# The last two batches of an attention-and-MoE kernel: first layer in three groups of 384 tokens in place of four of 288

## The chip, the core and the metric

The kernel runs on one core of a Trainium2 chip. The metric is the device time of one execution in microseconds (us); the time before is the median of three runs. A core has a matrix engine (TensorE, in the profile PE for the matmuls and PEld for the loads of their stationary operand), a vector engine (VectorE, DVE), a scalar engine (ScalarE, ACT), GpSimd (POOL), and SyncE (SP), which here issues all DMAs. Matmuls write to PSUM, eight banks of 512 fp32 columns in each of 128 partitions.

## The reference, cut

Four batches of 576 tokens with 8 heads of 64 pass a memory attention, then two MoE layers over all 2304 tokens:

```python
a = softmax(phi)                        # over 32 memory slots
k_m, v_m = a^T k, a^T v                 # per head: 32 x 64
attn = softmax(q k_m^T / 8) v_m         # per head: 576 x 64
x = attn as 2304 x 512
x = leaky_relu(x @ w_in) @ w_out        # first layer: 512 -> 2048 -> 512
out = mish(x @ w_in2) @ w_out2          # second layer
```

All inputs and the output are fp32.

## The kernel before

Every fp32 operand of the large matmuls is split into two float32r parts, hi and lo, and a product is three matmuls (hi hi, lo hi, hi lo) that add up in one PSUM bank. v_m is multiplied into w_in beforehand (the tiles vw, made in `vw_tasks`), so that the first layer's hidden block of 128 features needs, for a group of tokens, 2 head groups x 3 = 6 matmuls of vw on the attention weights `at`; that bank is h_t.

`stage1` writes one item: a group of 288 tokens (`NB1`, half a batch; `sub` is the half) and one block m of 128 of the 2048 hidden features. PE does the 6 matmuls into h_t (line 1226). ACT takes the leaky ReLU of it twice, as float32r (hi_t) and as fp32 (e_t, line 1240), and DVE subtracts the two (lo_t, line 1247). PE then multiplies with w_out (line 1259): for each of 4 blocks of 128 outputs, a PSUM bank acc_t each, hi with both parts of w_out (8 matmuls) and lo with the hi part (4 matmuls). An item is thus 18 matmuls, each with its own weight load and 288 columns. After the 16 items of a group the four acc_t are copied out as x_t or at_t (lines 312, 310 and 1304) and the next group takes the banks.

The first two batches pass in a turn that follows the decoding of the weights. The last two, which the change touches, pass group by group: batch 2 half 0, batch 2 half 1, batch 3 half 0, batch 3 half 1, 16 items each. What comes between them on PE is the attention of the next batch and its vw tiles (line 975: for a chunk of 512 features 8 small fp32 matmuls, which a trace shows as 16 records), copied to hi and lo by ACT and DVE (lines 310, 312 and 326). There are 8 vw buffers (`vw_tag`), 2 for each chunk of a batch.

The second layer (lines 1579 and 1791) works on groups of 384 tokens. Its operand is built by `split_x` on DVE and ACT in buffers `xt` that lie where the attention's buffers lay, so `split_x(0)` waits for the last user of those (`apool_users`, to which `keep` adds a task).

No order is written out by hand. Each piece of work is a task with the engines that may do it, an estimated cost and a priority, which is its place in a count of items; `Order.run` plays the tasks against the estimates and emits an instruction when its engine, its inputs and its buffers are free. K holds the offsets: S2 is the distance between the two halves of a batch's scores, XL how many items before the end of the first layer `split_x(0)` becomes due. The estimate for n matmuls of N columns is

```python
def mm(n, count=1):
    return count * (n / 2400 + 0.0133)
```

Of the kernel before, what the change touches and what calls it, by code (L numbers as in the profile page):

```python
# [23 lines left out]
def hop(a, b):  # L24
# [5 lines left out]

K = dict(
    LAG1=2, WIN=8, OB=2, RS=4, FILL=58, A1=10, S1=8.0,
    A2=30, S2=2.6, V1=2.4, V2=14, W2=45, W2S=3.8, O='phi0 kv0 phi1 q0 w0 kv1 q1 w1 w2 w3', HF0=-20.0, HF1=-7.0,
    HFD=0.3, TOP=0.1, HI=0.2, WO=2.0, WOL=1, WC=3.0, WC0=-38.0, V0=3.0, COLD=20, GL=1.5, AL=5.0, XL=22.0, T='0:1 0:1 1:2 0:2 1:2', SB=1,
    DW=280e3, DQ=1.3, DP=1.2, DS=0.78, DI=0.38, L4=0.5, L4P=1.6, L4S=0.8, L4T=5.0, MA=6, QL=4, PL=6, BH=(9,3,3,3,3), FK=-52.5, DWF=0.85, MV="......rvvrrvvrvr",
)

# [122 lines left out]
def kernel(  # L160
# [791 lines left out]

    win, win_ready, w_scr, w_loads = {}, {}, {}, [[] for _ in range(NC)]

    def vw_tasks(b, c, p0):
# [26 lines left out]

        t = keep(add(
            {"PE": 1.2}, p0, f, [x for g in range(NG) for x in vT[b, g][1] + win_ready[b, c, g]],
            pss + us, [vT[b, g][0] for g in range(NG)] + wbs,
        ))
        for g in range(NG):
            u, ps_b = us[g], pss[g]
            th, tl = hi_lo(
                p0 + 0.5 * g + 0.2, 512, lambda u=u: u.t[:, 0], lambda u=u: u.t[:, 1], lambda ps_b=ps_b: ps_b.t,  # L990
                [t], (), [u, ps_b], ps=True,
            )
            vw[b, c, g] = (u, th, tl)


# [70 lines left out]
    def next_batch(b):  # L1066
        d, st = (K["A1"], K["S1"]) if b == 1 else (K["A2"], K["S2"])
        p = base[b] - d
        kv_rest(b, p, 0.08 * d / 2)
        score_rest(b, p + 0.1 * d, (p + 0.3 * d, p + 0.3 * d + st), 0.03 * d)  # L1070

    def next_vw(b, c):
        vw_tasks(b, c, at_item["1", b, 0, 4 * c] - (K["V1"] if b == 1 else K["V2"]))

    for b, cs in chunk_turns:
        if b and not cs[0]:
            next_batch(b)
        for c in cs:
            if b:
                next_vw(b, c)  # L1080
                continue
            w_chunk(c)
            for m in range(4 * c, 4 * c + 4):
                wo_unit(m)


    kv_again = [kvq.new([P, 2, 1024]) for _ in range(2)]
    opened = [add({"SP": 0.0}, K["W2"], lambda e, x=x: x.make(), (), [x]) for x in kv_again]

    class View:  # L1090

# [14 lines left out]
            b.make = make  # L1106
            return b

    views = [View(j) for j in range(3)]
# [102 lines left out]
    def passes(n):  # L1212
        return [(j, wi) for j in range(n) for wi in range(2)]

    def stage1(i, b, sub, m):
        cols = slice(sub * NB1, (sub + 1) * NB1)
        c, j0 = m // 4, (m % 4) * P
        h = h_tag.new([P, NB1])
        us, ats = [vw[b, c, g] for g in range(NG)], [at[b, g] for g in range(NG)]
# [12 lines left out]
        t1 = add(  # L1232
            {"PE": mm(NB1, 6)}, i, f1, [x for u in us for x in u[1:]] + [x for u in ats for x in u[1 + sub]], [h],
            [u[0] for u in us + ats],
        )
        t1.main = i
        eb, hb, lb = e_tag.new([P, NB1]), hi_tag.new([P, NB1], F32R), lo_tag.new([P, NB1], F32R)

        def lrelu(o):
            nc.scalar.activation(out=o, in_=h.t, func=AF.Prelu, alpha=0.01)  # L1240


        t4 = add({"ACT": act(NB1, True)}, i + 0.3, lambda e: lrelu(hb.make()), [t1], [hb], [h])
        t3 = add({"ACT": act(NB1, True)}, i + 0.4, lambda e: lrelu(eb.make()), [t1, t4], [eb], [h])
        t5 = add(
            {"DVE": dve(NB1)}, i + 0.6,
            lambda e: nc.vector.tensor_tensor(out=lb.make(), in0=eb.t, in1=hb.t.bitcast(F32), op=ALU.subtract),  # L1247
            [t4, t3], [lb], [eb, hb],
        )
        first, last = m in firsts(b), m + 1 in firsts(b) + [NM]  # L1250
        if first:
            for kk in range(NK):
                accs[kk] = acc_tag.new([P, NB1])
        ac = dict(accs)
        wu = wo[m]

# [11 lines left out]
        if first:  # L1268
            for kk in range(NK):
# [13 lines left out]
        if last:  # L1283
            for kk in range(NK):
                tl = add(
                    {"PE": mm(NB1)}, i + LAG1 + 0.1 + 0.01 * kk, lambda e, kk=kk: mms([(kk, 0, 1)]),
                    [t5, *hs], (), [lb, wu[0], ac[kk]],
                )
                key = (b, kk // 2)
                fresh = key not in x1  # L1290
                if fresh:
                    if b < B - 1:
                        x1[key] = [x1_tag.new([P, 2, S]), {}]
                    else:
# [12 lines left out]

                deps = [tl] + [x for x in list(evs.values())[:1]]
                if add_in:
                    deps.append(evs[kk, sub])  # L1310
                evs[kk, sub] = add(
                    {"DVE": dve(NB1)} if add_in else {"ACT": act(NB1, True), "DVE": dve(NB1)},
                    i + LAG1 + 0.2, fe, deps, [xb] if fresh else [], [ac[kk]] if fresh else [ac[kk], xb],
                )
# [15 lines left out]

    slots = [
        (base[B - 1] + NM + x, t) for x, _, t in sorted(
            [(LAG1 + m, 0, wo_tag) for m in range(NM)] + [(4 * c + 3, 1, vw_tag) for c in range(NC) for _ in range(2)],
            key=lambda x: x[:2],
        )
    ]  # L1340
# [555 lines left out]
```

## Time and profile before

| | |
|---|---|
| median of 3 runs | 742.09 us (741.64 to 742.65) |
| the profiled execution | 741.87 us |
| its span, first to last instruction | 740.1 us |
| granted TensorE clock over the span | 0.999 |
| PE busy | 731.0 us, 99% of the span, 5875 matmul records |
| ACT, DVE busy | 402.5 us (54%), 550.6 us (74%) |
| first layer of batches 2 and 3 on PE, with what lies between | ends near 382 us |

The busy time of PE is the time in which at least one matmul is under way. Consecutive matmuls overlap, so the mean duration of one (297 ns for 288 columns) is not what one more of them costs. That is the distance from one start to the next in a dense stretch, called the pitch below: the length of a stretch divided by its matmuls.

### The profile page before, as it was taken

What the parts mean: (1) busy time and instruction counts of PE and PEld (TensorE: products, weight loads), DVE (VectorE), ACT (ScalarE), POOL (GpSimd) and SP (SyncE); (2) the same over time, 40 slices, a digit from 0 to 9 for tenths busy, and PEclk for the clock granted to TensorE, in tenths of its full rate; (3) what the DMA queues carried; (4) which work ended last, traced back from release to release, by engine and by line L of the source; (5) the groups of instructions that cost most, each with busy time, mean ns of one, the idle gap of its engine ahead of it and who ended that gap; (6) DMA issues with size and microseconds to landing.
All of it is one profiled execution on the core that took longest, in us unless ns stands there. A gap on an engine that the chain in (4) does not pass through costs nothing.

```text
span 740.1 us, 15587 instructions
## 1 busy us (share of the span) xinstructions
PE 731.0 (99%) x5875; PEld 701.3 (95%) x5875; DVE 550.6 (74%) x1153; ACT 402.5 (54%) x877; POOL 0.7 (0%) x6
## 2 busy tenths in 40 slices
PE   8999999999999999999999999999999999999997
PEld 7788899888999989999999999999999999999997
DVE  6899868598766965647859797867777966775595
ACT  4866458565553775645546665544464644444442
POOL 0000000000000000000000000000000000000000
PEclk9999999999999999999999999999999999999999
DMA  9793957787869587863559898788988778996475
GB/s 353 299 318 115 350 172 232 229 274 229 290 207 286 171 274 269 262 233 101 199 199 338 302 312 254 233 271 249 300 278 264 250 239 258 297 290 207 126 218 182
DMA packets 99322, 183.73 MB, mean 248 GB/s; under 512 B 8112, under 2 KB 51376, under 8 KB 99248
## 3 DMA queue, kind: packets, MB, share of 16 engines
q1 hardware_dynamic: 99248, 182.75, 75.5%
q8 instruction: 46, 0.75, 0.4%
q14 instruction: 28, 0.23, 0.1%
HBM read 140.25 MB, written 42.47 MB: 247 GB/s over the span
## 4 chain that ended last, share of the span: by engine, by line
PE 96%; DVE 2%; ACT 1%; DMA 0%; issue 0%
PE acc_t L1259 28%; PE h_t L1579 22%; PE acc_t L1791 22%; PE h_t L1226 13%; PE misc_t L1791 2%; PE misc_t L975 2%; PE acc_t L1579 2%; PE acc_t L508 1%; PE misc_t L741 1%; PE misc_t L646 1%; DMA phi_t<-in_phi_dram 0%; PE h_t L865 0%; ACT raws_t L369 0%; ACT raws_t L374 0%; PE misc_t L689 0%
## 5 line engine op out<-in xcount | busy, mean ns | idle before, releaser
L1259 PE MATMUL acc_t<-hi_t,wo_t 128*128 128x288 f32 x1024 | 160.6, 297 | 0.4 <-DVE x_t L312 0.3
L1259 PEld LDWEIGHTS acc_t<-hi_t,wo_t 128*128 128x128 f32 x1024 | 142.9, 188 | 12.2 <-issue 7.0
L1226 PE MATMUL h_t<-at_t,vw_t 128*128 128x288 f32 x768 | 123.1, 296 | 0.0
L1791 PE MATMUL acc_t<-hi_t,wo_t 128*128 128x384 f32 x448 | 114.4, 336 | 0.0
L1240 ACT ACTIVATE hi_t<-h_t 128x288 fp32r<-128x288 f32 x128 | 52.6, 411 | 111.8 <-PE acc_t L1259 105.3
L1226 PEld LDWEIGHTS h_t<-at_t,vw_t 128*128 128x128 f32 x768 | 108.5, 188 | 0.7 <-issue 0.6
L1247 DVE TENSOR_TENSOR lo_t<-e_t,hi_t 128x288 fp32r<-128x288 f32 x128 | 57.3, 450 | 47.4 <-ACT e_t L1240 21.6
L1259 PE MATMUL acc_t<-lo_t,wo_t 128*128 128x288 f32 x512 | 89.8, 297 | 0.5 <-DVE lo_t L1247 0.5
L1791 PEld LDWEIGHTS acc_t<-hi_t,wo_t 128*128 128x128 f32 x448 | 81.3, 188 | 0.0
L1259 PEld LDWEIGHTS acc_t<-lo_t,wo_t 128*128 128x128 f32 x512 | 74.7, 188 | 6.3 <-issue 5.6
L1579 PE MATMUL h_t<-xt_t,vw_t 128*128 128x384 f32 x396 | 79.4, 336 | 0.0
L1579 PE MATMUL h_t<-xt_t,wo_t 128*128 128x384 f32 x352 | 75.8, 336 | 0.0
L1791 PE MATMUL acc_t<-lo_t,wo_t 128*128 128x384 f32 x224 | 75.6, 337 | 0.0
L1758 DVE TENSOR_TENSOR lo_t<-wo_t,hi_t 128x384 fp32r<-128x384 f32 x94 | 52.0, 554 | 31.4 <-ACT hi_t L310 29.9
L1579 PEld LDWEIGHTS h_t<-xt_t,vw_t 128*128 128x128 f32 x396 | 69.3, 188 | 0.0
L310 ACT ACTIVATE hi_t<-wo_t 128x384 fp32r<-128x384 f32 x78 | 40.7, 524 | 40.7 <-PE acc_t L1791 36.4
L1579 PEld LDWEIGHTS h_t<-xt_t,wo_t 128*128 128x128 f32 x352 | 61.9, 188 | 0.0
L1240 ACT ACTIVATE e_t<-h_t 128x288 f32<-128x288 f32 x128 | 52.0, 406 | 0.0
L1791 PE MATMUL acc_t<-wo_t,hi_t 128*128 128x256 f32 x240 | 45.0, 282 | 0.0
L1604 ACT ACTIVATE wo_t<-wo_t 128x384 f32<-128x384 f32 x53 | 27.6, 522 | 30.8 <-DVE wo_t L1598 30.6
L1791 PEld LDWEIGHTS acc_t<-lo_t,wo_t 128*128 128x128 f32 x224 | 42.0, 188 | 0.0
L310 ACT ACTIVATE wo_t<-h_t 128x384 f32<-128x384 f32 x50 | 24.5, 489 | 31.1 <-PE h_t L1579 31.1
(263 smaller groups left out, 1110.0 us busy)
## 6 DMA issues: line engine op xcount, KB each, us to landing
wo_t<-tscr SPq DMA_DIRECT2D x168, 256.0 KB, 3.8
vw_t<-wsum SPq DMA_DIRECT2D x32, 512.0 KB, 4.7
win_t<-wscr SPq DMA_DIRECT2D x24, 512.0 KB, 5.5
raw_t<-in_moe_w_in_dram SPq DMA_DIRECT2D x19, 512.0 KB, 7.5
raw_t<-in_moe_w_out_dram SPq DMA_DIRECT2D x17, 512.0 KB, 5.5
wsum<-vw_t SPq DMA_DIRECT2D x16, 512.0 KB, 4.5
wo_t<-wsum SPq DMA_DIRECT2D x16, 512.0 KB, 4.3
tscr<-raw_t SPq DMA_DIRECT2D x9, 512.0 KB, 5.5
```

The source lines that it names most:

```text
L310: nc.scalar.activation(out=o, in_=i, func=AF.Copy)
L508: nc.tensor.matmul(out=acc.t[rows, :].rearrange("p (j d) -> p j d", j=2), lhsT=phv()[rows, r, :], rhs=kv.t[rows, :2304].rearrange("p (j r ...
L646: nc.tensor.matmul(out=accs_[g].t[o:o + M, :].rearrange("p (j d) -> p j d", j=2), lhsT=ph.t[rows, x, j, :], rhs=kv[g].t[rows, :, x % 2, j, :],
L975: nc.tensor.matmul(out=pss[g].t[M * (h ^ g):M * (h ^ g) + M, :], lhsT=vT[b, g][0].t[rows, g, h ^ g if b else h // 2, :], rhs=wbs[g].t[rows ...
L1226: nc.tensor.matmul(out=h.t, lhsT=us[g][0].t[:, wi, j0:j0 + P], rhs=ats[g][0].t[:, ai, cols], start=(n == 0), stop=(n == 3 * NG - 1),)
L1240: nc.scalar.activation(out=o, in_=h.t, func=AF.Prelu, alpha=0.01)
L1247: lambda e: nc.vector.tensor_tensor(out=lb.make(), in0=eb.t, in1=hb.t.bitcast(F32), op=ALU.subtract),
L1259: nc.tensor.matmul(out=ac[kk].t, lhsT=wu[0].t[:, wi, kk * P:(kk + 1) * P], rhs=(hb if src == 0 else lb).t, start=(first and (wi, src) == ( ...
L1579: nc.tensor.matmul(out=h.t, lhsT=w[:, wi, c0:c0 + P], rhs=xp[b, xi].ap()[:, j], start=(first and j == 0 and k3 == 0), stop=(j == 1 and k3 ...
L1604: lambda e: nc.scalar.activation(out=t_of[x](), in_=h.t if h else t_of[x](), func=AF.Mish),
L1758: lambda e, hb=hb, lb=lb, src=src: nc.vector.tensor_tensor(out=lb.make(), in0=src(), in1=hb.t.bitcast(F32), op=ALU.subtract),
L1791: nc.tensor.matmul(out=ac[t].t, lhsT=T[:, wi, t * P:(t + 1) * P] if wide else x.t[:, t * P:(t + 1) * P], rhs=x.t if wide else T[:, wi], st ...
```

## The change

The 64 items of 288 tokens of batches 2 and 3 become 48 items of 384 (`NB2`): group 0 is tokens 0 to 383 of batch 2, group 1 is the last 192 of batch 2 and the first 192 of batch 3, group 2 is tokens 192 to 575 of batch 3. The two parts of group 1 need different stationary tiles, so its items write h_t in two pieces of 192 columns with 6 matmuls each; from there on the item is one of 384 columns.

Group 1 needs the vw tiles of both batches. Chunk 0 of batch 3 goes into buffers of the attention (phi and the two T1, wrapped by `Two`); chunks 1 to 3 take the buffers of batch 2's chunks 0 to 2 once group 1 is through with them. The attention of batch 3 becomes due earlier with it, S2 and XL are new numbers (XL, in the same dict, goes from 22.0 to 18.0), and the places in which the second layer's tiles become free are renumbered. Nothing of batches 0 and 1 or of the second layer's matmuls is changed.

```diff
 K = dict(
-    A2=30, S2=2.6, V1=2.4, V2=14, W2=45, W2S=3.8, O='phi0 kv0 phi1 q0 w0 kv1 q1 w1 w2 w3', HF0=-20.0, HF1=-7.0,
...
+    A2=30, S2=3.5, V1=2.4, V2=14, W2=45, W2S=3.8, O='phi0 kv0 phi1 q0 w0 kv1 q1 w1 w2 w3', HF0=-20.0, HF1=-7.0,
...
-            us.append(vw_tag.new([P, 2, 512], F32R))
+            if b == B - 1 and not c and g:
+                us.append(Two([T_tag.new([P, 512], F32R) for _ in range(2)]))
+            else:
+                us.append((vw_tag if b < B - 1 or c else tags["phi"]).new([P, 2, 512], F32R))
...
-    items = [("1", b, sub, m) for b, m0, m1 in turns for sub in range(NSUB) for m in range(m0, m1)]
+    items = [("1", b, sub, m) for b, m0, m1 in turns for sub in range(NSUB) for m in range(m0, m1) if b < 2]
+    n_pair = len(items)
+    W3 = NB2 / NB1
+    for j in range(3):
+        parts = [(2, NB2 * j, min(NB2, S - NB2 * j))] if j < 2 else []
+        if j:
+            parts.append((3, 0 if j == 1 else S - NB2, NB2 if j == 2 else 2 * NB2 - S))
+        items += [("3", j, parts, m) for m in range(NM)]
...
-            n = 0
-            for g in range(NG):
-                for wi, ai in ((0, 0), (1, 0), (0, 1)):
-                    nc.tensor.matmul(
-                        out=h.t, lhsT=us[g][0].t[:, wi, j0:j0 + P], rhs=ats[g][0].t[:, ai, cols],
-                        start=(n == 0), stop=(n == 3 * NG - 1),
-                    )
-                    n += 1
+            o = 0
+            for x, (b, c0, n) in enumerate(parts):
+                for g in range(NG):
+                    for wi, ai in ((0, 0), (1, 0), (0, 1)):
+                        nc.tensor.matmul(
+                            out=h.t[:, o:o + n], lhsT=us[NG * x + g][0].t[:, wi, j0:j0 + P], rhs=ats[NG * x + g][0].t[:, ai, c0:c0 + n],
+                            start=((g, wi, ai) == (0, 0, 0)), stop=((g, ai) == (NG - 1, 1)), skip_group_check=True,
+                        )
+                o += n
...
+        if parts[-1][0] == B - 1 and not c:
+            keep(t1)
...
-    for i in range(n1):
-        stage1(i, *items[i][1:])
+    for i, (kind, x, y, m) in enumerate(items):
+        if kind == "1":
+            stage1(i, 1, [(x, y * NB1, NB1)], m)
+        else:
+            stage1(n_pair + W3 * (i - n_pair), W3, y, m)
```

Two places on PE show what this moves. The first is the item itself. Before, in a half of batch 3 (rows of PE in order; h is line 1226, acc line 1259):

```order
L1226 MATMUL h1_t_4309<-at_t_2573,vw_t_3092 128x288 x3
L1226 MATMUL h1_t_4309<-at_t_2581,vw_t_3093 128x288 x3
L1259 MATMUL acc0_t_3913<-lo_t_4261,wo12_t_1944 128x288
L1259 MATMUL acc1_t_3920<-lo_t_4261,wo12_t_1944 128x288
L1259 MATMUL acc2_t_3926<-lo_t_4261,wo12_t_1944 128x288
L1259 MATMUL acc3_t_3941<-lo_t_4261,wo12_t_1944 128x288
```

Now, the first item of group 1 (h is line 1262, acc line 1300; the acc rows are still group 0's):

```order
L1262 MATMUL h0_t_3815<-at_t_2618,vw_t_2579 128x192 x3
L1262 MATMUL h0_t_3815<-at_t_2624,vw_t_2580 128x192 x3
L1262 MATMUL h0_t_3815<-at_t_3476,phi_t_3596 128x192 x3
L1262 MATMUL h0_t_3815<-at_t_3478,T1_t_3597 128x192
L1262 MATMUL h0_t_3815<-at_t_3478,T1_t_3598 128x192
L1262 MATMUL h0_t_3815<-at_t_3478,T1_t_3597 128x192
L1300 MATMUL acc0_t_3352<-hi_t_3737,wo12_t_1944 128x384 x2
L1300 MATMUL acc1_t_3370<-hi_t_3737,wo12_t_1944 128x384 x2
```

The 6 matmuls of 288 columns have become 12 of 192 with 12 different weight loads, and the acc matmuls are of 384 columns.

The second place is where vw of a batch 3 chunk stands on PE (L975 before, L995 now). Before, the last chunk's 8 matmuls come early in group 3; the h rows behind them read other chunks, and the first that reads their result stands 118 rows further down:

```order
L975 MATMUL misc_t<-win_t,vTb_t 32x512 x8
L1259 MATMUL acc_t<-hi_t,wo_t 128x288 x8
L1226 MATMUL h_t<-at_t,vw_t 128x288 x6
L1259 MATMUL acc_t<-lo_t,wo_t 128x288 x4
L1226 MATMUL h_t<-at_t,vw_t 128x288 x6
```

Now, chunk 1 of batch 3 in group 1, behind the last h that reads chunk 0 of batch 2:

```order
L1300 MATMUL acc_t<-lo_t,wo_t 128x384
L995 MATMUL misc_t<-win_t,vTb_t 32x512 x8
L1300 MATMUL acc_t<-lo_t,wo_t 128x384 x3
L1300 MATMUL acc_t<-hi_t,wo_t 128x384 x8
L1300 MATMUL acc_t<-lo_t,wo_t 128x384 x4
L1262 MATMUL h_t<-at_t,vw_t 128x192 x12
```

Of those 12 the first 6 read batch 2, the last 6 the result of the L995 row. Between the two there are now 15 acc matmuls of 384 columns and those 6 of 192; at chunks 2 and 3 there are 20 and 6.

## Rows read from the trace of the kernel before

**Rows 1.** The page, part 1: busy time, share of the span, instructions of each engine.

```profile
PE 731.0 (99%) x5875; PEld 701.3 (95%) x5875; DVE 550.6 (74%) x1153; ACT 402.5 (54%) x877; POOL 0.7 (0%) x6
```

**Rows 2.** The page, part 4: chain that ended last, by engine.

```profile
PE 96%; DVE 2%; ACT 1%; DMA 0%; issue 0%
```

**Rows 3.** Page, part 5: line, operation, out<-in, count; busy, mean ns; idle before.

```profile
L1259 PE MATMUL acc_t<-hi_t,wo_t 128*128 128x288 f32 x1024 | 160.6, 297 | 0.4 <-DVE x_t L312 0.3
L1226 PE MATMUL h_t<-at_t,vw_t 128*128 128x288 f32 x768 | 123.1, 296 | 0.0
```

**Rows 4.** Stretches of PE alone: window, its length, busy (matmuls), clock, DMA.

```profile
308.00:374.00 66.00, 66.00 (x501) 1.00 0.56 192
440.00:500.00 60.00, 60.00 (x346) 1.00 0.81 258
```

**Rows 5.** Timeline of PE, 725 to 731: start, us, line, operation, tile, count.

```profile
724.92 0.40 PE L1791 MATMUL acc_t<-wo_t,hi_t 128*128 128x256 f32 x2
...
731.40 0.40 PE L1791 MATMUL acc_t<-wo_t,hi_t 128*128 128x256 f32 x2
```

**Rows 6.** Timeline, 30 and 214 us, and line 1057's durations (min/median/max): narrow matmuls.

```profile
29.73 2.84 PE L1057 MATMUL acc_t<-ident 128*128 128x128 f32 x24
...
L1057 PE MATMUL acc_t<-ident x116: 270/275/582, 1.4 to 37.7; 128*128 128x128 f32 x116
...
214.50 0.50 PE L623 MATMUL misc_t<-ones,rm_t 128*128 128x1 f32 x4
...
214.61 0.30 PEld L623 LDWEIGHTS misc_t<-ones,rm_t 128*128 128x128 f32 x2
...
214.72 0.19 PEld L623 LDWEIGHTS misc_t<-ones,rm_t 128*128 128x128 f32 x1
...
214.84 0.19 PEld L1259 LDWEIGHTS acc_t<-lo_t,wo_t 128*128 128x128 f32 x1
```

**Rows 7.** Timeline of PE and its loads about the wait at 307.5 us.

```profile
306.82 0.56 PE L1259 MATMUL acc_t<-lo_t,wo_t 128*128 128x288 f32 x3
...
307.53 0.53 PE L1259 MATMUL acc_t<-hi_t,wo_t 128*128 128x288 f32 x2 [0.16 <-DVE x_t L312]
...
307.53 0.30 PEld L1259 LDWEIGHTS acc_t<-hi_t,wo_t 128*128 128x128 f32 x2 [0.39 <-DVE x_t L312]
...
307.64 0.19 PEld L1259 LDWEIGHTS acc_t<-hi_t,wo_t 128*128 128x128 f32 x1
307.77 0.19 PEld L1226 LDWEIGHTS h_t<-at_t,vw_t 128*128 128x128 f32 x1
```

**Rows 8.** Timeline, all engines, 285 to 289 us: one vw chunk of batch 3.

```profile
285.22 1.09 PE L975 MATMUL misc_t<-win_t,vTb_t 64*32 64x512 f32 x16
...
286.44 0.69 DVE L312 CAST vw_t<-misc_t 128x512 fp32r<-128x512 f32 x1 [2.44 <-PE misc_t L975]
...
287.12 0.46 DVE L1247 TENSOR_TENSOR lo_t<-e_t,hi_t 128x288 fp32r<-128x288 f32 x1
287.50 1.28 DVE L326 TENSOR_TENSOR vw_t<-misc_t,vw_t 128x512 fp32r<-128x512 f32 x2
```

**Rows 9.** Groups of instructions by line and shape: matmuls of fp32, not float32r.

```profile
L975 PE MATMUL misc_t<-win_t,vTb_t 64*32 64x512 f32 x240 | 16.3, 601 | 0.0
```

**Rows 10.** Timeline of DVE: first of the second layer's xt, and two later steps.

```profile
332.67 0.56 DVE L312 CAST xt_t<-x_t 128x768 fp32r<-128x768 f32 x1
...
349.68 0.56 DVE L1539 TENSOR_TENSOR raw_t<-raw_t,x_t 128x384 f32<-128x384 f32 x1
...
357.41 0.96 DVE L326 TENSOR_TENSOR wo_t<-raw_t,xt_t 128x768 fp32r<-128x768 f32 x1 [0.18 <-ACT xt_t L310]
```

**Rows 11.** Stretches of DVE alone: window, its length, busy (instructions), clock, DMA.

```profile
222.00:307.00 85.00, 58.02 (x113) 1.00 0.80 255
308.00:382.00 74.00, 48.62 (x97) 1.00 0.53 185
```

More of the change, by code (lines that the diff above doesn't have):

```diff
@@ L953, with __init__, make, __getitem__ @@
     win, win_ready, w_scr, w_loads = {}, {}, {}, [[] for _ in range(NC)]
+    class Two:
+        def __init__(self, bufs):
+            self.bufs = bufs
+        def make(self):
+            for x in self.bufs:
+                x.make()
+            self.t = self
+        def __getitem__(self, key):
+            return self.bufs[key[1]].t[key[:1] + key[2:]]
+    def bufs_of(us):
+        return [y for x in us for y in (x.bufs if isinstance(x, Two) else [x])]
     def vw_tasks(b, c, p0):
@@ L1065 @@
         score_tasks(0, g, -59.5 + 10 * g, (-54.0, K["HF0"]) if not g else (-40.0, K["HF1"]), K["HFD"])
[L1066 to L1088, printed above, removed]
+    kv_again, opened = [], []
     class View:
@@ L1107, in new, with next_batch, next_vw @@
             return b
-    views = [View(j) for j in range(3)]
+    views = []
+    def next_batch(b):
+        d, st = (K["A1"], K["S1"]) if b == 1 else (K["A2"], K["S2"])
+        p = base[b] - d
+        kv_rest(b, p, 0.08 * d / 2)
+        score_rest(b, p + 0.1 * d, (p + 0.3 * d, p + 0.3 * d + st), 0.03 * d)
+    def next_vw(b, c):
+        vw_tasks(b, c, chunk_at(b, c) - (K["V1"] if b == 1 else K["V2"]))
+    for b, cs in chunk_turns:
+        if b and not cs[0]:
+            next_batch(b)
+            if b == B - 1:
+                kv_again += [kvq.new([P, 2, 1024]) for _ in range(2)]
+                opened += [add({"SP": 0.0}, K["W2"], lambda e, x=x: x.make(), (), [x]) for x in kv_again]
+                views += [View(j) for j in range(3)]
+        for c in cs:
+            if b:
+                next_vw(b, c)
+                continue
+            w_chunk(c)
+            for m in range(4 * c, 4 * c + 4):
+                wo_unit(m)
     more = Ring(raw.slots + rawm.slots[3:])
@@ L1213, in passes, with stage1 @@
         return [(j, wi) for j in range(n) for wi in range(2)]
-    def stage1(i, b, sub, m):
-        cols = slice(sub * NB1, (sub + 1) * NB1)
+    def stage1(i, step, parts, m):
+        N, b0 = sum(n for _, _, n in parts), parts[0][0]
         c, j0 = m // 4, (m % 4) * P
-        h = h_tag.new([P, NB1])
-        us, ats = [vw[b, c, g] for g in range(NG)], [at[b, g] for g in range(NG)]
+        h = h_tag.new([P, N])
+        us = [vw[b, c, g] for b, _, _ in parts for g in range(NG)]
+        ats = [at[b, g] for b, _, _ in parts for g in range(NG)]
@@ L1232, in stage1 @@
+        halves = [[sub for sub in range(NSUB) if c0 < (sub + 1) * NB1 and c0 + n > sub * NB1] for _, c0, n in parts for g in range(NG)]
         t1 = add(
-            {"PE": mm(NB1, 6)}, i, f1, [x for u in us for x in u[1:]] + [x for u in ats for x in u[1 + sub]], [h],
-            [u[0] for u in us + ats],
+            {"PE": sum(mm(n, 6) for _, _, n in parts)}, i, f1,
+            [x for u in us for x in u[1:]] + [x for u, hs in zip(ats, halves) for sub in hs for x in u[1 + sub]], [h],
+            bufs_of([u[0] for u in us + ats]),
@@ L1245, in stage1 @@
+        t3 = add({"ACT": act(N, True)}, i + 0.4, lambda e: lrelu(eb.make()), [t1, t4], [eb], [h])
         t5 = add(
-            {"DVE": dve(NB1)}, i + 0.6,
+            {"DVE": dve(N)}, i + 0.6,
             lambda e: nc.vector.tensor_tensor(out=lb.make(), in0=eb.t, in1=hb.t.bitcast(F32), op=ALU.subtract),
@@ L1249, in stage1 @@
         )
-        first, last = m in firsts(b), m + 1 in firsts(b) + [NM]
+        lag = LAG1 * step
+        first, last = m in firsts(b0), m + 1 in firsts(b0) + [NM]
         if first:
             for kk in range(NK):
-                accs[kk] = acc_tag.new([P, NB1])
+                accs[kk] = acc_tag.new([P, N])
         ac = dict(accs)
@@ L1309, in stage1, with fe @@
[L1309 to L1314, printed above, removed]
+                o = 0
+                for b, c0, n in parts:
+                    key = (b, kk // 2)
+                    fresh = key not in x1
+                    if fresh:
+                        x1[key] = [x1_tag.new([P, 2, S]) if b < B - 1 else at_tag.new([P, 2, S]), {}]
+                    xb, evs = x1[key]
+                    add_in = (kk, c0) in evs
+                    def fe(e, kk=kk, xb=xb, fresh=fresh, add_in=add_in, o=o, c0=c0, n=n):
+                        if fresh:
+                            xb.make()
+                        src, x = ac[kk].t[:, o:o + n], xb.t[:, kk % 2, c0:c0 + n]
+                        if add_in:
+                            nc.vector.tensor_tensor(out=x, in0=src, in1=x, op=ALU.add)
+                        else:
+                            copy(e, x, src)
+                    deps = [tl] + [x for x in list(evs.values())[:1]]
+                    if add_in:
+                        deps.append(evs[kk, c0])
+                    evs[kk, c0] = add(
+                        {"DVE": dve(n)} if add_in else {"ACT": act(n, True), "DVE": dve(n)},
+                        i + lag + 0.2, fe, deps, [xb] if fresh else [], [ac[kk]] if fresh else [ac[kk], xb],
+                    )
+                    o += n
```

50 lines of the change are left out of this document (19 added, 31 removed).

## The prediction

> **What bounds the kernel now.** I read the page first: PE is busy for 99% of the span [rows 1], and the chain that ended last lies on PE for 96% [rows 2]. DVE and ACT have a quarter of their time or more free. So the kernel is as long as its matmuls, and the question is what one matmul costs. The groups of part 5 don't say: 297 ns is the mean time from the start of one to its end [rows 3], and neighbours overlap. The pitch comes from dense stretches. From 308 to 374 us there are only matmuls of 288 columns: 66 us hold 501 records, of which two or three only reach in over the left edge, so the pitch is 66 / 498.5 = 132.4 ns. From 440 to 500 us there are only matmuls of 384 columns: 346 records, two of them over the edge, 60 / 344 = 174.4 ns [rows 4]. For 256 columns the timeline of the end runs from 724.92 to 731.40 us with 54 matmuls between the two starts (18 times the pattern of 2 and 1): 120.0 ns [rows 5]. The granted clock is 1.00 in these stretches, the 2.4 GHz level, at which the columns alone take 120, 160 and 106.7 ns: each matmul pays 12 to 14 ns on top. That is where a change to fewer, wider matmuls can gain, and 13.3 ns is what the planner's `mm` has for it.
>
> **The change, part by part.** *Removed:* 64 items of 18 matmuls of 288 columns, 1152 x 132.4 ns = 152.5 us of PE. *Added, wide:* of each of the 16 blocks m, 12 h matmuls (groups 0 and 2) and 36 acc matmuls of 384 columns, 768 x 174.4 ns = 133.9 us. *Added, narrow:* group 1 has 12 h matmuls of 192 columns for each m, 192 in all. Nothing in the first layer or the second is of float32r with fewer than 256 columns, so their pitch has to be bounded. The break-even is (152.5 - 133.9) / 192 = 97 ns.
>
> The lower end is the columns plus the surcharge, 80 + 13 = 93 ns: 17.9 us, a sum of -0.7 us. But every matmul loads its own stationary tile, and the rows show what a load costs that isn't covered. The two fp32 matmuls of line 623 have a single column; the trace records each as two passes. Their four loads and the next one follow at 214.61, 214.72 and 214.84 us, 0.11 to 0.12 us apart, although next to nothing streams [rows 6]. The warm-up matmuls, 128 columns, run 24 in 2.84 us: with the last one's own 0.275 us off (the median of one), 23 pitches of 111.5 ns [rows 6]. These are fp32 tiles; a float32r tile behaves alike. Behind the wait at 307.5 us a load starts at 307.53, the next at 307.64, 0.11 us later, and only the one after that is back at the pitch, 0.13 us on [rows 7]: a load starts when the matmul before it starts, and takes some 108 ns. Behind 256 columns or more that is hidden, 120 against 111. Behind 192 columns it isn't. I take 112 ns, the pitch of the rows in which a load of the same 128 x 128 tile is what the next matmul waits for: 192 x 112 = 21.5 us.
>
> The upper end is a float32r matmul that would stream no faster than plain fp32: the 16 records of one vw chunk take 1.09 us as two sets of eight side by side [rows 8], one record being 0.60 us [rows 9], so a set of 512 columns holds the array for 0.5 us, 0.97 ns a column, and 192 columns would take 187 ns: 35.9 us, a sum of +17.3 us. I see no reason for it in the rows of 256 to 384 columns, which are proportional to the columns.
>
> **Sum on PE:** 133.9 + 21.5 - 152.5 = +2.9 us. At 120 ns, if the surcharge came on top of the load, it would be +4.4 us.
>
> The Trainium skill ("TensorE: Matmul & The Clock Gate", section "Back-to-back issue gap") gives a warm gap of N / 2.4 + 2.5 ns, by the columns alone. By it the change would save 192 gaps of 2.5 ns, 0.5 us, as an estimate. The trace does not agree on the size: 132.4 ns for 288 columns against 122.5.
>
> *ACT and DVE:* two ACT and one DVE pass over each h become 48 sets of wider ones for 64, a little less work in all; both have room (DVE 58 of 85 us and 49 of 74 us in the stretches concerned [rows 11]). Cost nothing, hidden behind PE.
>
> *Copying acc out:* one group boundary less. Before, one boundary made PE wait, at 307.5 us: three matmuls that start at 306.82 (the last of them by the pitch at 307.08) are followed at 307.53, 0.45 us in place of 0.13, and the first load is uncovered, 0.11 us: 0.4 us in all, the idle time of the whole group [rows 3, 7]. Between groups 1 and 2 the first hi matmul again stands right behind the four lo, so I expect that wait to remain. Zero.
>
> *vw of batch 3, chunks 1 to 3:* the same matmuls, later. The 8 stand on PE as before, at the same price. What they hand on is new: the copies must be through before the h that reads them, behind 15 acc matmuls and 6 of 192 columns (15 x 0.174 + 6 x 0.112 = 3.3 us) at chunk 1 and 20 and 6 (4.2 us) at chunks 2 and 3. In the trace the chunk's matmuls start at 285.22 and last 1.09 us, and DVE ends the second subtraction at 288.78: 2.5 us behind the last matmul, with one lo_t of 0.46 us in between [rows 8]. 2.5 us fit into 3.3. DVE's queue at chunk 1 holds an acc copy in place of that lo_t, about the same. Zero, with the cover named; the loads of w_in for the next chunk go out on SP when the buffer is free, some 4 items (13 us) ahead.
>
> *split_x(0)* now has to wait for the last h that reads phi and T1, m = 3 of group 2. Twelve items of 18 x 0.174 = 3.1 us are left then, 38 us. Before, it ran from 332.67 to 358.4 us, 26 us, in the gaps of DVE and ACT [rows 10]. It fits. The second layer's first products stand where they stood, between the last acc rows.
>
> **Which value.** Span 740.1 + 2.9 = 743.0; the profiled execution was 741.87, that is 1.8 us more than its span and 0.2 less than the median, so the median is 742.1 + 2.9 = **745.0 us**.
>
> **The rivals.** *(1) No floor under the narrow matmul.* If the loads run ahead by more than one, 192 columns cost 93 ns, and with the wait at the boundary gone as well the time is 742.1 - 0.7 - 0.4 = 741.0: not slower. It decides from a pitch below 97 ns. For it: PE's pitch follows the columns at 256, 288 and 384. Against: [rows 6, 7], where a load never starts before the matmul ahead of it. The Trainium skill's gap formula cited above is a rule of this kind.
> *(2) New waits.* The copies of vw at chunks 1 to 3 come late because DVE is behind: one more pass of 0.7 to 1.2 us ahead of them uses up the slack of 0.8 us at chunk 1, and a load of w_in that lands late does so at any of the three. A wait of 0.5 to 1 us at each adds 2 us: 747.0. For it: the distance on PE shrank from a whole group to one or two items. Against: slack of 0.8, 1.7 and 1.7 us in the rows.
> *(3) Narrow float32r streams at fp32's rate:* 742.1 + 17.3 = 759.4. For it: nothing narrower than 256 columns is in the trace, as if avoided. Against: the columns' proportionality.
>
> **How the numbers follow.** Floor of 108 to 120 ns with few new waits 0.68 (743.7 to 747), rival 2 0.14 (746 to 749), rival 1 0.11 (740.3 to 742.3), rival 3 0.07. The range 743.0 to 749.0 holds the first two, 0.8 of the chance. A measurement of this kernel tells 0.2%, 1.5 us, from no change: slower means above 743.6. Rival 1 is mostly within 0.2%, with a third of it below 740.6; some 0.04 of the first case lies within. Faster 0.04, same 0.11, slower 0.85.
>
> **What would show it.** In the profile after, consecutive 192-column matmuls of line 1262 start 110 to 115 ns apart and their loads fill the time (PE busy as before); group 1's items last 12 x 0.112 + 12 x 0.174 = 3.4 us against 3.1 us of group 0's. The 384-column items of groups 0 and 2 run at 174 ns. The second layer begins 3 us later and takes as long as before. Starts 93 ns apart make rival 1 right and me wrong by sign; idle PE ahead of h in group 1, with DVE or a DMA named, makes it rival 2; starts 160 ns or more apart make it rival 3.

## The result, and the profile after

The changed kernel takes **746.12 us** (median of 6 runs, 745.16 to 746.80), the kernel before in the same series 742.37 us (6 runs, 741.14 to 742.85): ratio 1.0053, 95% interval 1.0040 to 1.0066. A second series gave 746.26 to 742.42 us, ratio 1.0049 (1.0035 to 1.0063). The change costs 3.8 us; 2.9 were forecast, and 746.12 us lies in the stated range of 743.0 to 749.0.

The page of the changed kernel, parts 1, 4 and 5, against [rows 1 to 3]:

```profile
PE 735.9 (99%) x5683; PEld 704.5 (95%) x5683; DVE 550.9 (74%) x1138; ACT 399.4 (54%) x844; POOL 0.7 (0%) x6
...
PE 95%; ACT 1%; DVE 1%; DMA 1%; issue 0%; SPq 0%
...
L1300 PE MATMUL acc_t<-hi_t,wo_t 128*128 128x288 f32 (+1 forms) x896 | 158.1, 316 | 0.3 <-DVE x_t L312 0.2
...
L1262 PE MATMUL h_t<-at_t,vw_t 128*128 128x288 f32 (+2 forms) x720 | 116.5, 300 | 0.0
```

PE has 192 matmuls fewer and is busy 4.9 us longer; it bounds the kernel as before. So fewer matmuls do not make less work, and the reason must lie in what one costs. The timeline of PE over an item and a half of group 1 shows it:

```profile
279.33 0.81 PE L1262 MATMUL h_t<-at_t,vw_t 128*128 128x192 f32 x6
279.98 0.50 PE L1262 MATMUL h_t<-at_t,phi_t 128*128 128x192 f32 x3
280.31 0.50 PE L1262 MATMUL h_t<-at_t,T_t 128*128 128x192 f32 x3
280.65 0.36 PE L1300 MATMUL acc_t<-lo_t,wo_t 128*128 128x384 f32 x1
...
284.95 1.48 PE L1262 MATMUL h_t<-at_t,vw_t 128*128 128x192 f32 x12
286.26 1.07 PE L1300 MATMUL acc_t<-hi_t,wo_t 128*128 128x384 f32 x5
```

Twelve matmuls of 192 columns take 280.65 - 279.33 = 1.32 us, and 286.26 - 284.95 = 1.31 us: 110 ns each, not 93. (The duration of a row runs to the end of its last matmul; the pitch is read from the starts.) The trace has 192 of them with a sum of 21.05 us. The wide matmul behind such a dozen is followed after some 200 ns in place of 174: 16 times 26 ns, 0.4 us. Together 21.5 us.

Stretches of PE alone, with the columns of [rows 4] (a dozen narrow ones, then 384 columns in the second layer and in group 2):

```profile
279.33:280.64 1.31, 1.31 (x13) 1.00 0.99 400
...
440.00:500.00 60.00, 60.00 (x345) 1.00 0.81 251
345.00:372.00 27.00, 27.00 (x158) 1.00 0.46 164
```

The first row has one record that reaches in from the left, the other two have two each. The wide matmuls of the first layer run at 27 / 156 = 173 ns, those of the second layer at 60 / 343 = 175, and the granted clock is 1.00 throughout.

The sum over PE from the first instruction that differs (160.24 us before, 161.19 after) to the last acc matmul of the first layer (389.08 and 393.87): 228.84 us before, 232.69 after, **+3.85 us**. (The end near 382 us that the table of the time before gives for the first layer is too early: rows of the second layer stand between the first layer's from 374 us on, and its last acc matmul is the one at 389.08.) Behind it the second layer takes 345.8 us in both. The first changed instruction stands 0.95 us later in the changed kernel; that arises in the first 20 us, ahead of it, and differs from trace to trace: the same point of the second profile of the changed kernel stands at 160.56 us. From there its sum is 233.37 us, 0.68 more than in the first profile, by the longer stall that is shown below as the third wait.

Three waits of the change are in the trace. The first is at the start of the second vw chunk of batch 3, which now stands between two items of group 1 (timeline, all engines):

```profile
282.07 0.60 ACT L310 ACTIVATE vw_t<-misc_t 128x512 fp32r<-128x512 f32 x1 [0.53 <-PE misc_t L995]
282.16 0.69 DVE L312 CAST vw_t<-misc_t 128x512 fp32r<-128x512 f32 x1 [3.25 <-PE misc_t L995]
282.42 0.36 PEld L1300 LDWEIGHTS acc_t<-hi_t,wo_t 128*128 128x128 f32 x2
282.56 0.87 ACT L310 ACTIVATE x_t<-acc_t 128x384 f32<-128x384 f32 x2
...
283.10 1.00 PEld L1300 LDWEIGHTS acc_t<-hi_t,wo_t 128*128 128x128 f32 x6 [0.32 <-ACT x_t L310]
283.23 1.28 DVE L326 TENSOR_TENSOR vw_t<-misc_t,vw_t 128x512 fp32r<-128x512 f32 x2
```

ACT copies a vw tile first and only then, from 282.56, the acc bank of group 0; PE needs that bank for the first item of group 1 and its load stands until 283.10. By the starts this is 0.28 us of PE. The copies of vw themselves are through at 284.51, and the h that reads them starts at 284.95 without a wait: the cover that the prediction named held.

The second lies ahead of the attention of batch 3, where DVE adds the four acc banks of a half of one of the first two batches to x_t. Before, the four adds run in a row (timeline of DVE):

```profile
177.70 1.54 DVE L1304 TENSOR_TENSOR x_t<-acc_t,x_t 128x288 f32<-128x288 f32 x4
```

Now a pass of batch 2's attention, which stood at 172.57 us before and at 172.89 with the two numbers alone (below), stands between the first and the second (timelines of DVE and of PE):

```profile
177.97 0.39 DVE L1344 TENSOR_TENSOR x_t<-acc_t,x_t 128x288 f32<-128x288 f32 x1
178.28 0.74 DVE L781 TENSOR_TENSOR T_t<-T_t,sm_t 128x576 f32<-128x576 f32 x1
178.95 1.18 DVE L1344 TENSOR_TENSOR x_t<-acc_t,x_t 128x288 f32<-128x288 f32 x3
```

```profile
178.43 0.53 PE L1300 MATMUL acc_t<-hi_t,wo_t 128*128 128x288 f32 x2
178.79 0.96 PE L1262 MATMUL h_t<-at_t,vw_t 128*128 128x288 f32 x6
179.59 1.13 PE L1300 MATMUL acc_t<-hi_t,wo_t 128*128 128x288 f32 x6
180.55 0.70 PE L1300 MATMUL acc_t<-lo_t,wo_t 128*128 128x288 f32 x4
```

The eight hi matmuls take 0.36 and 0.96 us from start to start, 1.33 in place of 8 x 0.132 = 1.06, and the three loads that come late start 0.04 us behind the end of an add, at 178.42, 179.82 and 180.18 us. By the starts this is 0.27 us, in both profiles of the changed kernel.

The third is in the attention of batch 3, which the change brings forward from 218 us to 200 us (timeline of PE; first the changed kernel in the first profile, then in the second):

```profile
200.13 2.23 PE L646 MATMUL misc_t<-kvq_t,phi_t 64*32 64x128 f32 x143
202.53 0.27 PE L646 MATMUL misc_t<-kvq_t,phi_t 64*32 64x128 f32 x1 [0.17 <-issue]
```

```profile
199.48 2.23 PE L646 MATMUL misc_t<-kvq_t,phi_t 64*32 64x128 f32 x143
202.59 0.27 PE L646 MATMUL misc_t<-kvq_t,phi_t 64*32 64x128 f32 x1 [0.88 <-issue]
```

These are 144 equal matmuls of one task; 143 run and the last one stands still with no semaphore to wait for. Before, the 144 run through in 2.18 us; here they take 2.60 and 3.31 us. The late one starts at 202.5 to 202.6 us whether PE arrives early or late, so a program that is ahead by 0.65 us at 160 us has lost that lead at 203. What it waits for isn't shown: "issue" is all the profile says. In the 199th to 201st us a packet of an instruction queue moves (it has one in all three profiles of this order), so a late piece of program is the nearest candidate, argued and not shown. The kernel before has such a packet at 198.90 us as well, and in the four variants below whose order differs, where the 144 start between 201.2 and 210.6 us, no two of them stand more than 0.09 us apart.

### The profile page after: what moved, and what is told of

Same layout as the page of the kernel before. It is cut to its first block, busy times and chain, and to the rows that moved or that the text cites. A ratio compares the mean times of both kernels' runs of the same rounds, so it can differ in the third digit from the quotient of the medians.

```text
span 744.8 us, 15138 instructions
## 1 busy us (share of the span) xinstructions
PE 735.9 (99%) x5683; PEld 704.5 (95%) x5683; DVE 550.9 (74%) x1138; ACT 399.4 (54%) x844; POOL 0.7 (0%) x6
## 4 chain that ended last, share of the span: by engine, by line
PE 95%; ACT 1%; DVE 1%; DMA 1%; issue 0%; SPq 0%
PE acc_t L1300 28%; PE h_t L1624 22%; PE acc_t L1836 21%; PE h_t L1262 14%; PE misc_t L1836 2%; PE misc_t L995 2%; PE acc_t L1624 2%; PE acc_t L508 1%; DMA kvq_t<-in_q_dram 1%; PE misc_t L741 1%; PE misc_t L646 1%; PE h_t L865 0%; ACT raws_t L369 0%; ACT raws_t L374 0%; PE misc_t L689 0%
## 5 line engine op out<-in xcount | busy, mean ns | idle before, releaser
L1300 PE MATMUL acc_t<-hi_t,wo_t 128*128 128x288 f32 (+1 forms) x896 | 158.1, 316 | 0.3 <-DVE x_t L312 0.2
L1262 PE MATMUL h_t<-at_t,vw_t 128*128 128x288 f32 (+2 forms) x720 | 116.5, 300 | 0.0
L1280 ACT ACTIVATE hi_t<-h_t 128x288 fp32r<-128x288 f32 (+1 forms) x112 | 50.0, 446 | 115.8 <-PE acc_t L1300 109.8
L1287 DVE TENSOR_TENSOR lo_t<-e_t,hi_t 128x288 fp32r<-128x288 f32 (+1 forms) x112 | 55.0, 495 | 52.1 <-PE acc_t L1300 24.9
L1624 PE MATMUL h_t<-xt_t,wo_t 128*128 128x384 f32 x424 | 90.1, 336 | 0.0
L1300 PE MATMUL acc_t<-lo_t,wo_t 128*128 128x288 f32 (+1 forms) x448 | 87.3, 316 | 0.5 <-DVE lo_t L1287 0.5
L1624 PEld LDWEIGHTS h_t<-xt_t,wo_t 128*128 128x128 f32 x424 | 74.7, 188 | 0.0
L1624 PE MATMUL h_t<-xt_t,vw_t 128*128 128x384 f32 x324 | 65.4, 336 | 0.0
L1280 ACT ACTIVATE e_t<-h_t 128x288 f32<-128x288 f32 (+1 forms) x112 | 49.4, 441 | 0.0
L1803 DVE TENSOR_TENSOR lo_t<-vw_t,hi_t 128x384 fp32r<-128x384 f32 x50 | 27.7, 555 | 18.3 <-ACT hi_t L310 17.7
```

The lines of the kernel that those rows point to most:

```text
L1262: nc.tensor.matmul(out=h.t[:, o:o + n], lhsT=us[NG * x + g][0].t[:, wi, j0:j0 + P], rhs=ats[NG * x + g][0].t[:, ai, c0:c0 + n], start=((g, ...
L1300: nc.tensor.matmul(out=ac[kk].t, lhsT=wu[0].t[:, wi, kk * P:(kk + 1) * P], rhs=(hb if src == 0 else lb).t, start=(first and (wi, src) == ( ...
L1624: nc.tensor.matmul(out=h.t, lhsT=w[:, wi, c0:c0 + P], rhs=xp[b, xi].ap()[:, j], start=(first and j == 0 and k3 == 0), stop=(j == 1 and k3 ...
L1803: lambda e, hb=hb, lb=lb, src=src: nc.vector.tensor_tensor(out=lb.make(), in0=src(), in1=hb.t.bitcast(F32), op=ALU.subtract),
```

## The experiments

Theory 1 is the prediction's: a load of a 128x128 stationary tile takes some 110 ns, runs beside one matmul only, and is the floor under 192 columns. Theory 2 is that there is no such floor and the new order makes the loss.

**The floor, by itself.** Behind the last instruction of the kernel before stand 24 matmuls of each width on one stationary tile.

```diff
+PROBES = [(384, 128), (288, 128), (256, 128), (240, 128), (224, 128), (192, 128), (160, 128), (128, 128), (64, 128), (192, 64), (128, 64), (192, 32)]
...
+        for n_, m_ in PROBES:
+            for r_ in range(24):
+                nc.tensor.matmul(
+                    out=pr_[:m_, :n_], lhsT=pw[:, :m_], rhs=pw[:, :n_], start=True, stop=True, skip_group_check=True,
+                )
```

> The kernel before, with a tail of 288 more float32r matmuls behind its last instruction: 24 in a row for each number of columns, all with the same 128x128 stationary tile (the last three sets with 64 or 32 stationary columns). Theory 1 (a load of the stationary tile that takes 108 to 112 ns and runs beside one matmul only): start to start 174 ns at 384 columns, 132 at 288, 120 at 256, then 112 to 114 at 240, and flat, 108 to 114, at 224, 192, 160, 128 and 64. Theory 2 (columns and 13 ns, no floor): 113 at 240, 107 at 224, 93 at 192, 80 at 160, 67 at 128, 40 at 64. Theory 3 (narrow float32r streams at the rate of fp32): about 187 at 192 columns, 218 at 224, 125 at 128. What no row says is what the number of stationary columns does: if the load goes by them, 192 columns with 64 stationary ones cost 93 ns, the columns and 13, and 128 columns 67 ns or a little more; if it doesn't, both stand at 112. The tail adds some 32 us to the kernel under theory 1.

Measured in one run, from the first start of a train to its last, divided by 23, at a granted clock of 1.00:

| columns | stationary columns | ns from start to start |
|---|---|---|
| 384 | 128 | 173.3 |
| 288 | 128 | 131.7 |
| 256 | 128 | 119.4 |
| 240 | 128 | 112.1 |
| 224, 192, 160, 128 | 128 | 111.3, 111.1, 111.1, 111.2 |
| 192 | 32 | 88.6 |
| 128 | 64 | 60.0 |

Flat from 240 columns down: theory 1. Within the trains from 224 to 128 the loads start every 111.7 ns. The last two rows say what the floor depends on: with fewer stationary columns 192 columns cost 89 ns and 128 columns 60, so the price of a load falls with its stationary columns. The Trainium skill ("TensorE: Matmul & The Clock Gate", section "LDWEIGHTS (loading the stationary operand)") has a load go by its stationary columns, columns / 1.2 ns, which is an estimate of 106.7 ns for 128; the trace agrees in kind and has 111.7 from one load to the next.

In the trains of 64 columns, and of 192 with 64 stationary ones behind it, the granted clock was not 1.00. The stretches of these two and of the next (window, length, PE busy and count, PEld, DVE, ACT, POOL, granted clock, DMA share, GB/s):

```profile
758.70:761.40 2.70, 2.70 (x25) 2.70 (x24) 0.00 (x0) 0.00 (x0) 0.00 (x0) 0.92 0.00 0
761.75:765.00 3.25, 3.25 (x25) 3.25 (x26) 0.00 (x0) 0.00 (x0) 0.00 (x0) 0.60 0.00 0
765.10:766.40 1.30, 1.30 (x25) 1.30 (x24) 0.00 (x0) 0.00 (x0) 0.00 (x0) 1.00 0.06 13
```

That raised a question for any kernel with many narrow matmuls: do waits for loads bring the clock down? A longer tail, 180 of each of four widths, in one run:

```diff
+PROBES = [(192, 128), (128, 128), (64, 128), (384, 128)]
...
+            for r_ in range(180):
```

> The kernel before with a longer tail: 180 float32r matmuls in a row of each of 192, 128, 64 and 384 columns, all with a 128x128 stationary tile. In the tail of 24 each, starts were 112 ns apart from 224 columns down to 64, and late in the train of 64 columns the granted clock fell to the 1.2 GHz level; it was back after some 3 us of 192 columns with a smaller tile. If a train of matmuls that wait for their loads brings the clock down whatever their columns, the trains of 192 and 128 show it too, with starts 215 ns apart (the 401 ns loads of that stretch), and a kernel with many of them in a row would pay double. If only very short streams do, the first two stay at 112 ns and 1.00, and only the train of 64 falls. In the train of 384 the clock comes back in either case. No theory of the change hangs on it: there only 12 narrow ones stand in a row.

The same view of it: a stretch of 192, of 128, of 64 and of 384 columns.

```profile
735.20:755.20 20.00, 20.00 (x181) 20.00 (x181) 0.92 (x3) 0.00 (x0) 0.00 (x0) 1.00 0.13 40
755.50:775.40 19.90, 19.90 (x181) 19.90 (x180) 0.00 (x0) 0.00 (x0) 0.00 (x0) 1.00 0.00 1
...
785.00:790.00 5.00, 5.00 (x26) 5.00 (x25) 0.00 (x0) 0.00 (x0) 0.00 (x0) 0.50 0.00 0
...
820.00:845.00 25.00, 25.00 (x145) 24.70 (x143) 0.00 (x0) 0.00 (x0) 0.00 (x0) 1.00 0.00 1
```

20 us of 192 columns and 20 us of 128 keep 1.00, at 111.5 ns a matmul. Of 64 columns the first 20 or so run at 112 ns, then the clock is at 0.50, the 1.2 GHz level, and a matmul takes 213.3 ns, nearly twice as long. (The 401 ns that the expectation gives for the loads of the first tail are the durations of the matmuls there; a load at 0.50 lasts 333 to 338 ns.) Under 384 columns it is back after 3.5 us.

**One batch in group 1.** The changed kernel with its 192 narrow matmuls as 96 wide ones on vw of batch 2 alone (half of batch 3's part of the first layer is left out), all else in place and PE's order the same:

```diff
-            for x, (b, c0, n) in enumerate(parts):
+            for x, (b, c0, n) in enumerate(parts if len(parts) == 1 else [(2, S - N, N)]):
```

> The changed kernel, in which group 1 reads vw of batch 2 alone, with 6 h matmuls of 384 columns for 12 of 192 (half of batch 3's part of the first layer is left out, the instructions around it stay): 96 x 174.4 = 16.7 us in place of 192 x 112 = 21.5 us. Theory 1 (the narrow matmuls carry the loss): 4.8 us less than the changed kernel, 741.3 us by its median of 746.1, so 1 us under the kernel before. Theory 2 (192 columns cost 93 ns, and the loss is new waits): 1.1 us less, 745.0. A wait that stays in group 1 (the one of 0.3 us at the first chunk) is in both.

741.98 us (10 runs, 740.31 to 744.70; ratio to before 0.9999, 0.9988 to 1.0010), 4.1 to 4.3 us under the changed kernel; theory 1 said 4.8, theory 2 1.1. The traces agree better: from the matmul behind the L646 stall to the last one, 537.10 us in the changed kernel and 532.31 here, 4.8 us. One item of it on the timeline of PE:

```profile
278.51 1.23 PE L1262 MATMUL h_t<-at_t,vw_t 128*128 128x384 f32 x6
279.58 0.34 PE L1300 MATMUL acc_t<-lo_t,wo_t 128*128 128x384 f32 x1
```

1.07 us for the six, against 1.32 for the twelve. So the width of these 192 matmuls carries the loss, and the order that stayed the same, with waits of its own, costs no more than the wide groups bring in.

**The old order, only narrower.** The kernel before, with the h matmuls of one half batch cut in two, no instruction moved:

```diff
+    CUTS = {(b, sub): [(0, 288)] for b in range(B) for sub in range(NSUB)}
+    CUTS[3, 0] = [(0, 144), (144, 288)]
...
+                    for x, y in CUTS[b, sub]:
+                        nc.tensor.matmul(
+                            out=h.t[:, x:y], lhsT=us[g][0].t[:, wi, j0:j0 + P], rhs=ats[g][0].t[:, ai, sub * NB1 + x:sub * NB1 + y],
```

> The kernel before, with the h matmuls of batch 3's first half alone cut from 288 into two of 144 columns (96 become 192; nothing else is changed, no instruction moves). Theory 1 (floor of 112 ns under a matmul): 192 x 112 - 96 x 132.4 = +8.8 us, 751.2 us. Theory 2 (columns and 13 ns): 192 x 73.3 - 96 x 132.4 = +1.4 us, 743.8 us. Theory 3 (fp32's rate, 0.97 ns a column): 192 x 140 - 96 x 132.4 = +14.2 us, 756.6.

751.11 us (ratio 1.0118, 1.0103 to 1.0133), +8.8 us where theory 1 said +8.8 and theory 2 +1.4. (The two halves begin their sums in turn in one bank, so that this half batch's sums are given up; what counts here is the number and shape of the matmuls.) On its timeline twelve take 321.79 - 320.50 = 1.29 us, 108 ns each, where 144 columns at 2.4 GHz alone are 60:

```profile
320.50 1.46 PE L1230 MATMUL h_t<-at_t,vw_t 128*128 128x144 f32 x12
321.79 1.26 PE L1263 MATMUL acc_t<-hi_t,wo_t 128*128 128x288 f32 x8
```

**The planner's two numbers alone.**

```diff
-    A2=30, S2=2.6, V1=2.4, V2=14, W2=45, W2S=3.8, O='phi0 kv0 phi1 q0 w0 kv1 q1 w1 w2 w3', HF0=-20.0, HF1=-7.0,
-    HFD=0.3, TOP=0.1, HI=0.2, WO=2.0, WOL=1, WC=3.0, WC0=-38.0, V0=3.0, COLD=20, GL=1.5, AL=5.0, XL=22.0, T='0:1 0:1 1:2 0:2 1:2', SB=1,
+    A2=30, S2=3.5, V1=2.4, V2=14, W2=45, W2S=3.8, O='phi0 kv0 phi1 q0 w0 kv1 q1 w1 w2 w3', HF0=-20.0, HF1=-7.0,
+    HFD=0.3, TOP=0.1, HI=0.2, WO=2.0, WOL=1, WC=3.0, WC0=-38.0, V0=3.0, COLD=20, GL=1.5, AL=5.0, XL=18.0, T='0:1 0:1 1:2 0:2 1:2', SB=1,
```

> The kernel before with only the two numbers of the planner that the change sets (S2 3.5 for 2.6, XL 18 for 22). Theory 1: the work on PE is the same, and PE is busy 99% of the span, so 742.4 us within 0.2%. The rival, that these numbers have a part in the loss by waits that they add: 743.5 us or more, with idle PE ahead of a line of batch 2 or 3.

741.73 us, ratio 0.9988 (0.9979 to 0.9998): by themselves, in the old order, they cost nothing.

**The changed kernel again, and groups without a narrow matmul.** Groups of 336, 480, 336 and of 320, 512, 320 tokens have middle halves of 240 and 256 columns, just over the floor. The second:

```diff
+    NBA = 320
...
-        parts = [(2, NB2 * j, min(NB2, S - NB2 * j))] if j < 2 else []
+        parts = [(2, NBA * j, min(NBA, S - NBA * j))] if j < 2 else []
...
-            parts.append((3, 0 if j == 1 else S - NB2, NB2 if j == 2 else 2 * NB2 - S))
+            parts.append((3, 0 if j == 1 else S - NBA, NBA if j == 2 else S - NBA))
...
-    e_tag = Ring([Slot(pipe, f"e{j}") for j in range(3)])
-    hi_tag = Tag(pipe, "hi", 3)
-    lo_tag = Tag(pipe, "lo", 3)
+    e_tag = Ring([Slot(pipe, f"e{j}") for j in range(2)])
+    hi_tag = Tag(pipe, "hi", 2)
+    lo_tag = Tag(pipe, "lo", 2)
```

> The changed kernel once more, in more rounds beside the kernel before and the two variants of this series. By the traces its first layer is 3.85 us longer from the first changed PE instruction to its end, so 746.2 us, ratio 1.005. If a good part of the first difference had come from the start of the program, which is 0.5 to 1.3 us different from trace to trace, the ratio would be nearer to 1.004.

> The change with groups of 336, 480 and 336 tokens, so that the two halves of the middle group have 240 columns, where the tail of probes had 112 ns, the columns' own price, and not the load's. To fit, the rings e and hi have two buffers for three. Per block m: 36 matmuls of 336 columns, 12 of 240 and 12 of 480, at 153.4, 112.1 and 216.4 ns (on the line of 132.4 at 288 and 174.4 at 384, 0.4375 ns a column): 9.46 us, 151.4 us for the 16, against 152.5 before and 155.4 changed. Theory 1 (the loss is the load's floor under 192 columns): 1.1 us under the kernel before, with some 0.9 us of new waits 742.2 us, 4 us under the changed kernel. Theory 2 (the loss lies in the new order, its copies of vw and its two-buffer View, not in the width): no better than the changed kernel, 745 us or more. Rival to both: two buffers for three make PE wait at every item, 744 us or more with idle PE ahead of the acc or h lines.

> The same with groups of 320, 512 and 320 tokens: halves of 256 columns. The rings e, hi and lo have two buffers for three. Per block m: 36 matmuls of 320 columns, 12 of 256 and 12 of 512, at 146.4, 119.7 and 230.4 ns: 9.47 us, 151.5 us for the 16. Theory 1: 742.3 us, as with 336 and 480, within 0.2% of the kernel before. If every matmul cost its columns at 2.4 GHz and a fixed 13.3 ns, as the planner has it, the twelve matmuls fewer would be worth 12 x 13.3 x 16 = 2.6 us: 740.7 with the same waits. Theory 2: 745 or more. Waits from the two-buffer rings: 744 or more, with idle PE in the second layer too.

746.26, **751.60** and **750.13 us** (ratios 1.0049, 1.0125, 1.0103). The two variants are slower than the changed kernel, as the rival said that the thinner rings would make them. The middle items themselves are as planned: twelve of 256 columns take 291.58 - 290.14 = 1.44 us, 120 ns each.

```profile
290.14 1.60 PE L1263 MATMUL h_t<-at_t,vw_t 128*128 128x256 f32 x12
291.58 1.09 PE L1301 MATMUL acc_t<-lo_t,wo_t 128*128 128x512 f32 x4
```

So the rings had to be priced alone: the changed kernel with the same rings and its own widths.

> The changed kernel (384, 384, 384) with two buffers for three in the rings e and hi: the control of the variant with 336, 480 and 336 tokens, which differs from it in the widths alone. That one measured 751.6 us; in its trace the second layer takes 352.3 us for 345.8 in the changed kernel. Theory 1 (the widths gain 155.4 - 151.4 = 4.0 us, the rings lose some 9): the control is slower still, 755.6 us, with a second layer of 352.3 us too, so that the whole difference lies in the last two batches of the first layer. Theory 2 (the widths gain nothing, and the loss of the change is in its order): 751.6 us, the same. If the rings cost nothing and the widths themselves lose: 746.

> The changed kernel with two buffers for three in the rings e, hi and lo: the control of the variant with 320, 512 and 320 tokens (750.1 us). Theory 1: 750.1 + 155.4 - 151.5 = 754.0 us, the difference again in the last two batches of the first layer. Theory 2: 750.1. If the rings cost nothing: 746.

752.41 us (ratio 1.0136) with two buffers in e and hi, 752.06 us (1.0133) in all three. The rings cost 6 us, not 9, most of it in the second layer. In 338 us of it PE does 2079 matmuls in the changed kernel, 2051 in the variant with 320 and 512 and 2045 in its control (PE alone, one row of each kernel, in this order):

```profile
396.00:734.00 338.00, 338.00 (x2079) 1.00 0.82 259
```

```profile
396.00:734.00 338.00, 336.94 (x2051) 1.00 0.80 259
```

```profile
396.00:734.00 338.00, 337.03 (x2045) 1.00 0.81 260
```

Against their controls the widths then gain 1.9 us with 320 and 512 (3.1 us between the last matmuls of the two traces) and 0.8 us with 336 and 480 (0.9 in the traces), where 3.9 and 4.0 were expected. The first agrees with theory 1 in sign and, by the trace, nearly in size (the h and acc matmuls of batches 2 and 3 add up to 154.5 us in the variant and 157.4 in its control): by the measured pitches (146.7, 118.9 and 232.7 ns) it saves 155.4 - 152.0 = 3.4 us of PE. The second gain, 0.8 us, is smaller than what the intervals of the two ratios can tell apart (1.0109 to 1.0141 and 1.0119 to 1.0153). There the matmuls are cheaper by 3.3 us as well, but its trace has 1.7 us more of waits than its control, half of them in batches 0 and 1, where the two differ in the planner's order alone. Why, was not settled. A version with wide halves and full rings was not tried, as the rings had given way to the wider tiles; by the pitches it would be 0.5 us of PE under the kernel before, at best too little to be told from it.

## Why the prediction was right, point by point

*What bounds the kernel:* PE, before and after.

*The narrow matmuls,* the open term, 192 x 112 = 21.5 us: measured 21.05, and 0.4 in the wide matmuls behind the dozens, 21.5. The price was taken from the rows in which a load of the same tile is what the next matmul waits for [rows 6, 7]; the tail of probes gave 111.1 to 111.7 ns for it. Rival 1 (93 ns) and rival 3 (187 ns) fall: 93 ns would need a smaller stationary tile (88.6 ns with 32 columns), and there is no rate of its own for narrow float32r. The gap formula that the prediction sets beside rival 1 is given in that section of the Trainium skill ("TensorE: Matmul & The Clock Gate", "Back-to-back issue gap") for a matmul without its load; of a stream of loads and matmuls the section says that both set the spacing, and with 110 ns at 192 columns, against 82.5 as an estimate by the formula, the trace agrees.

*The terms with a price from dense stretches:* removed 152.5, in the trace 153.6; wide 133.9, in the trace 135.6. Both have the small losses at each change to fp32 matmuls and back on top, which a pitch from a dense stretch leaves out, and the waits named here.

*What was set to zero and wasn't:* this is the step that was off, 0.95 us in all, the sum being +3.85 us and not +2.9. It stayed inside the range, which had room for it without naming these waits. The copying out of acc was to cost nothing new. The wait at the boundary between groups 1 and 2 remained, as said; on the timeline of PE the hi matmuls stand back from 339.17 (four lo at the pitch) to 339.44:

```profile
338.47 0.86 PE L1300 MATMUL acc_t<-lo_t,wo_t 128*128 128x384 f32 x4
339.44 0.89 PE L1300 MATMUL acc_t<-hi_t,wo_t 128*128 128x384 f32 x3
```

But between groups 0 and 1 a vw chunk now stands at the place where the banks are emptied, and ACT took the vw tile first: 0.28 us. The prediction had looked at who waits for the vw copies, and not at who waits behind them. DVE's work, said to be hidden behind PE, wasn't all of it: a pass of the attention came between the adds that empty the acc banks, 0.27 us. And the attention of batch 3 was moved by 18 us and met the stall in L646, 0.42 us in the first profile and 1.1 us in the second. No row of before shows it. These three make 0.97 us; one more change to fp32 matmuls and small differences in the pitches cancel within 0.05.

*Rival 2,* waits at the vw chunks, was right in kind at the first chunk alone, by another engine's queue and another tile, and at 0.28 us in place of 0.5 to 1 at each of three. New waits elsewhere make some 1 us with it, half of the 2 us that it added.

*split_x(0)* was to cost nothing: DVE's casts of x_t run at 352.92 and 353.38 us, 20 us later than in [rows 10], and the second layer takes 345.76 us against 345.80.

*The absolute time* came out 1.1 us over the forecast: 0.3 of it is the base, whose median was 742.09 us in the three runs ahead of the forecast and 742.37 in six, and the rest is the term above.

## What to carry to other kernels

In these runs a matmul costs the larger of its stream and the load of the next stationary tile. Before columns are regrouped, compare each new width with the point at which the two are equal (here 240 columns for a 128x128 float32r tile); whatever falls under it is paid at the floor, and a few such matmuls use up what the wide ones save. When a copy is moved, or its place in an engine's queue changes, look at what that engine has queued behind it as well as at who waits for the copy.

## What the runs showed of the hardware

- Between the floor and a full bank the price of a matmul is nearly proportional to its columns: 119.4 ns at 256, 131.7 at 288, 146.7 at 320, 173.3 at 384, 218.8 at 480, 232.7 at 512 (320, 480 and 512 from the traces of the two variants, the others from the tail), that is 0.45 to 0.47 ns a column. What is over the 2.4 GHz of the columns is 12 ns at 288, 13 at 384 and 19 at 512, so the planner's fixed 13.3 ns overstates what merging saves. From 288 to 384 columns a column gets cheaper by 1.3%.
- The load's floor falls with the stationary columns (128 columns take 111.2 ns with 128 of them and 60.0 with 64), and it goes with the clock: 111.7 ns at a granted clock of 1.00, 213.3 at 0.50.
- A train of 180 matmuls of 128 columns at the floor, 20 us, had a granted clock of 1.00, the 2.4 GHz level, throughout; in the train of 64 columns behind it the clock went to 0.50, the 1.2 GHz level, after some 20 matmuls, 2.3 us.
- A run of 144 equal matmuls can stop before its last one with no semaphore named, at the same time of the program in three profiles, and take back a lead that was gained before it.
